# Softmax by column blocks, a fused pass for both norms, row sums in two banks and another order of the G/H products

## The chip, the cores and the metric

The kernel runs on one core of a Trainium2 chip. The metric is the device time of one execution in microseconds (us). TensorE (PE) does the matmuls and PEld its weight loads, VectorE (DVE) and ScalarE (ACT) the elementwise work, GpSimd (POOL) issues most loads. Spans in a profile are some 2 us shorter than the device time of the same run.

## The reference

```python
qn = q / (norm(q, axis=1) + 1e-6); kn = k / (norm(k, axis=1) + 1e-6)   # q, k, v: 4 x 6016 x 256
s = kn.transpose(0, 2, 1) @ qn / tau                                   # 256 x 256 per batch
a = exp(s - max(s)); a /= a.sum(-1) + 1e-9
x = (v @ a).reshape(24064, 256)
out = (sigmoid(x @ w_gate) * (x @ w_val)) @ w_out                      # 256 -> 1536 -> 256
```

The kernel never forms x. It multiplies the small matrix `a` into the weights, G = a w_gate and H = a w_val, once per batch, and then runs a gated MLP from v directly.

## The kernel before

A batch is cut into 12 blocks (ci) of up to 512 tokens, a block into 12 slots (f), each of two gate and two value matmuls (the prediction calls the slots of the first block GLU blocks). Scores, norms, softmax and G/H of the next batch are put into the slots of the present one ("side work"); those of batch 0 run ahead of everything. The parts that matter:

```python
psg = pool("psg", 2, space=PSUM)      # ps_gate: two banks
psv = pool("psv", 2, space=PSUM)      # ps_val: two banks
pso = pool("pso", 2, space=PSUM)
pss = pool("pss", 1, space=PSUM)      # scores of the next batch: one bank
psm = pool("psm", 1, space=PSUM)      # norms, row sums and G/H products: one bank
# ...
def scale_k(b):                       # two passes of 128x256
    for j in range(CB):
        nc.vector.tensor_tensor(out=x, in0=x, in1=s["rk"], op=ALU.mult)
def exps(b):                          # the query norm goes in as the scale
    for j in range(CB):
        nc.scalar.activation(out=s["e"][:, j, :], in_=s["x"][:, j, :], func=ACT.Exp, bias=shift, scale=s["r"][:, j : j + 1])
# ... side work of a transition (next batch n, during blocks 10 and 11)
at(10 * FC + 1, norms_inv, n)
at(10 * FC + 2, spread_k, n)          # four matmuls that spread the key norms over rows: ps_rk
for j in range(CB):
    at(10 * FC + 1, copy_s, n, j)     # scores out of their bank
at(10 * FC + 4, scale_k, n)
at(10 * FC + 11, exps, n)
at(11 * FC + 0, sums, n)              # row sums into psm
for i in range(len(gh_order)):
    at(11 * FC + i, gh, n, i)         # twelve G/H products, all through psm
```

In a slot the order on TensorE is gate (2 matmuls), value (2), 4 matmuls of the previous block's output (in blocks 9 and 10 of batches 0 to 2 they come in one go at the end of the block), then the side work. The value product is evicted by one DVE pass, hT = ps_val x g_sb.

Of the kernel before, what the change touches and what calls it, by code (L numbers as in the profile page):

```python
# [9 lines left out]
FP32 = mybir.dt.float32  # L10
BF16 = mybir.dt.bfloat16
ACT = mybir.ActivationFunctionType
ALU = mybir.AluOpType
# [4 lines left out]
def kernel(  # L18
# [68 lines left out]
    def mm(out, lhsT, rhs, start, stop, **kw):  # L87
        nc.tensor.matmul(out, lhsT=lhsT, rhs=rhs, start=start, stop=stop, **kw)  # L88
# [74 lines left out]
    def squares(b, t0, nt, which, engine):  # L163
        src = qk[b, t0][which]
        sq = sqpool.tile([P, TPC, C], BF16, tag=f"sq{which}", name=f"sq{which}")
        if engine is nc.scalar:
            nc.scalar.activation(out=sq[:, :nt, :], in_=src[:, :nt, :], func=ACT.Square)  # L167
        else:
            engine.tensor_tensor(  # L169
                out=sq[:, :nt, :], in0=src[:, :nt, :], in1=src[:, :nt, :], op=ALU.mult  # L170
            )
        return sq

    def norm_mms(ps, sqs, nt, first, last):

        for w, sq in enumerate(sqs):
            for u in range(nt):
                for j in range(CB):
                    mm(
                        ps[:, w * CB + j : w * CB + j + 1],  # L180
                        sq[:, u, ds(j * P, P)],
                        ones_bf[:, 0:1],
                        start=(first and w == 0 and u == 0 and j == 0),
                        stop=(last and u == nt - 1),
                        skip_group_check=True,
                    )
# [59 lines left out]
            s["x"] = attp.tile([P, CB, C], FP32, tag="x", name="x_sb")  # L246
        nc.vector.tensor_copy(out=s["x"][:, j, :], in_=s["s"][:, j, :])

    def scale_k(b):
        s = st[b]  # L250
        for j in range(CB):
            x = s["x"][:, j, :]
            nc.vector.tensor_tensor(out=x, in0=x, in1=s["rk"], op=ALU.mult)  # L253

    def exps(b):
        s = st[b]
        s["e"] = attp.tile([P, CB, C], BF16, tag="e", name="e_sb", bufs=2)
        for j in range(CB):
            nc.scalar.activation(
                out=s["e"][:, j, :],  # L260
                in_=s["x"][:, j, :],
                func=ACT.Exp,
                bias=shift,
                scale=s["r"][:, j : j + 1],
            )

    def sums(b):
        s = st[b]
        ps_r = psm.tile([P, CB], FP32, tag="m", name="ps_r")
        for i in range(CB):  # L270
            for j in range(CB):
                mm(
                    ps_r[:, i : i + 1],
                    s["e"][:, j, ds(i * P, P)],
                    ones_bf[:, 0:1],
                    start=(i == 0 and j == 0),
                    stop=(j == CB - 1),
                    skip_group_check=True,
                )
        r = attp.tile([P, CB], FP32, tag="rrow", name="rrow", bufs=2)  # L280
        nc.vector.tensor_scalar(out=r, in0=ps_r, scalar1=1e-9, scalar2=None, op0=ALU.add)  # L281
        nc.vector.reciprocal(r, r)
        s["rrow"] = r
        s["gh"] = [
            [ghpool.tile([P, CB, FG], BF16, tag=f"{n}{fg}", name=f"gh_{n}{fg}") for fg in range(NFG)]
            for n in ("G", "H")
        ]

    gh_order = [(fg, w, i) for fg in range(NFG) for w in range(2) for i in range(CB)]

    def gh(b, n, pl=None, tag=None, act=0):
        s = st[b]
        fg, w, i = gh_order[n]
        ps = (pl or psm).tile([P, FG], FP32, tag=tag or "m", name="ps_gh")
        for j in range(CB):
            mm(
                ps,
                s["e"][:, j, ds(i * P, P)],
                w_sb[w][fg][:, j, :],
                start=(j == 0),  # L300
                stop=(j == CB - 1),
            )
        dst = s["gh"][w][fg][:, i, :]
        r = s["rrow"][:, i : i + 1]
        if n % 2 == act:
            nc.scalar.activation(out=dst, in_=ps, func=ACT.Copy, scale=r)  # L306
        else:
            nc.vector.tensor_scalar(out=dst, in0=ps, scalar1=r, scalar2=None, op0=ALU.mult)  # L308
# [1 line left out]

    vts = {}

    def transpose_v(b, ci, ps=None):

        t0, nt = groups[ci]
        v_sb = vs.pop((b, ci))
        vT = vtpool.tile([P, TPC * CB, P], BF16, tag="vT", name="vT")
        flat = v_sb[:, :nt, :].rearrange("p t c -> p (t c)")
        if ps is None:
            nc.sync.dma_start_transpose(out=vT[:, : nt * CB, :], in_=flat)  # L320
        else:
            for n in range(nt * CB):
                nc.tensor.transpose(
                    out=ps[:, n, :], in_=flat[:, ds(n * P, P)], identity=ident_bf
                )
            nc.vector.tensor_copy(out=vT[:, : nt * CB, :], in_=ps[:, : nt * CB, :])
        vts[b, ci] = vT.rearrange("p (u cb) n -> p cb u n", cb=CB)

    hts = {}
# [61 lines left out]
    for g in range(last0 + 2):  # L391
        if g <= last0:
            t0, nt = groups0[g]
            sq[g] = (
                squares(0, t0, nt, 0, nc.vector),
                squares(0, t0, nt, 1, nc.vector if g == last0 else nc.scalar),
            )
            for u in range(nt):
                score(0, t0, u)
        if g >= 1:  # L400
            norm_mms(ps_n0, sq.pop(g - 1), groups0[g - 1][1], g == 1, g == last0 + 1)
    st[0]["n"] = ps_n0
    norms_sqrt(0)
    nc.scalar.preload_act_table(ACT.Exp)
# [2 lines left out]
    copy_s(0, 1)  # L407
    busy(12)
    spread_k(0)
    busy(10)  # L410
    scale_k(0)
    transpose_v(0, 0, psv.tile([P, TPC * CB, P], BF16, tag="v", name="ps_tp"))
    exps(0)
    nc.scalar.preload_act_table(ACT.Sigmoid)
    sums(0)
    for n in range(4):
        gh(0, n, *((psg, "g"), (psv, "v"))[n % 2], act=1)


    def side_work(b):  # L420

        side = {}

        def at(slot, fn, *a):
            side.setdefault(divmod(slot, FC), []).append((fn, a))

        for ci in range(NCH):
            nb, nci = (b, ci + 1) if ci + 1 < NCH else (b + 1, 0)
            lb, lci = (b, ci + 2) if ci + 2 < NCH else (b + 1, ci + 2 - NCH)
            if (nb, nci) == (0, 1):  # L430
                at(7, lambda: transpose_v(0, 1, psm.tile([P, TPC * CB, P], BF16, tag="m", name="ps_tp")))
            elif nb < B:
                at(ci * FC + 2, transpose_v, nb, nci)
            if lb < B:
                at(ci * FC + 0, load_v, lb, lci)
        n = b + 1
        if n == B:
            return side
        first, last = (14 if b == 0 else 0), 9 * FC
        for g, (t0, nt) in enumerate(groups):  # L440
            s0 = first + g * (last - first) // NCH
            at(max(0, s0 - 20), load_qk, n, t0, nt)
            for u in range(nt):
                at(first + (t0 + u) * (last - first) // NT, score, n, t0, u)
            if g == 0:
                at(s0, acc_start, n)
            for i, (fn, w) in enumerate(((acc_square, 0), (acc_add, 0), (acc_square, 1), (acc_add, 1))):
                at(s0 + 1 + 2 * i, fn, n, g, w)
        at(9 * FC + 10, norms_mm, n)
        at(9 * FC + 11, norms_sqrt, n)  # L450
        at(10 * FC + 1, norms_inv, n)
        at(10 * FC + 2, spread_k, n)
        for j in range(CB):
            at(10 * FC + 1, copy_s, n, j)
        at(10 * FC + 4, scale_k, n)
        at(10 * FC + 11, exps, n)
        at(11 * FC + 0, sums, n)
        for i in range(len(gh_order)):
            at(11 * FC + i, gh, n, i)
        return side  # L460


# [1 line left out]
    for b in range(B):  # L464
        side = side_work(b)
        for ci in range(NCH):
            block = b + 1 < B and ci in (9, 10)
            for f in range(FC):
                glu(b, ci, f)
                flush()  # L470
                if prev is not None and not block:
                    out_mms(*prev, f * TPC, (f + 1) * TPC)
                for fn, a in side.get((ci, f), ()):
                    fn(*a)
                if (b, ci) == (0, 0) and f < len(gh_order) - 4:
                    gh(0, 4 + f, pso, "o", act=1)
            if prev is not None and block:
                for s in range(TPC):
                    out_mms(*prev, s * FC, (s + 1) * FC)
                    flush()  # L480
            prev = (b, ci)
# [38 lines left out]
```

## Time and profile before

| | before |
|---|---|
| time, median of the first 3 runs | 840.12 us |
| same kernel, all its later runs beside the experiments | 838.78 to 841.92 us |
| profiled span | 838.0 us |
| PE / DVE / ACT busy | 97% / 68% / 47% |

The prediction shows the views that carry the argument. A busy row of PE is drawn over the start of the next one: a pair of 512-column matmuls is 0.59 us long, though the next pair starts after 0.433 us.

### The profile page before, as it was taken

How to read it: one execution, taken by the hardware profiler on the slowest of the kernel's cores; microseconds unless marked ns; L12 is line 12 of the kernel's file. 1: busy time of each engine (PE TensorE's matmuls, PEld its weight loads, DVE VectorE, ACT ScalarE, POOL GpSimd, SP SyncE). 2: the span in 40 equal slices, each digit the busy share in tenths (PEclk: the TensorE clock that was granted, in tenths of full speed). 3: DMA queues.
4: the chain of work that ended last, by engine and by line, in shares of the span. 5: the costliest groups of instructions: out<-in, count | busy, mean ns of one | idle time of the engine just before them, and what ended most of it. 6: DMA issues, size and time to landing. Idle time of an engine off the chain costs nothing.

```text
span 838.0 us, 14001 instructions
## 1 busy us (share of the span) xinstructions
PE 817.0 (97%) x5338; PEld 506.6 (60%) x5338; DVE 566.3 (68%) x977; ACT 390.6 (47%) x640; POOL 83.2 (10%) x159
## 2 busy tenths in 40 slices
PE   5899999999999999999999999999999999999998
PEld 4646666665666666665565666666566556665666
DVE  2377777776667777777656777777756666666664
ACT  4554444445644444444554444444654444444442
POOL 5532100002011100000210020000000000000000
PEclk9799999999999999999999999999999999999999
DMA  9999624226655443223864453223222422322211
GB/s 209 206 205 186 124 51 89 61 51 136 125 102 107 101 102 63 54 51 85 153 132 83 92 118 80 51 73 67 60 48 51 95 51 73 78 50 65 49 36 69
DMA packets 78739, 77.18 MB, mean 92 GB/s; under 512 B 50769, under 2 KB 55633, under 8 KB 78673
## 3 DMA queue, kind: packets, MB, share of 16 engines
q0 software_dynamic: 23920, 38.81, 28.0%
q1 hardware_dynamic: 54608, 36.97, 15.8%
q8 instruction: 41, 0.67, 0.3%
q10 hardware_dynamic: 144, 0.52, 0.2%
q14 instruction: 26, 0.20, 0.1%
HBM read 78.64 MB, written 24.64 MB: 123 GB/s over the span
## 4 chain that ended last, share of the span: by engine, by line
PE 91%; DMA 3%; DVE 2%; ACT 1%; issue 1%; POOL 0%; ACTq 0%; POOLq 0%
PE ps_o L88 29%; PE ps_gate L88 28%; PE ps_val L88 28%; PE ps_s L88 4%; DMA k_sb<-in_k_dram 3%; PE ps_gh L88 2%; DVE hT L351 1%; ACT g_sb L350 1%; PE ps_rk L88 0%; DVE out_sb L377 0%; ACT gh_H L306 0%; PE ps_n L88 0%; DVE gh_H L308 0%; DVE gh_G L308 0%; DVE x_sb L253 0%
## 5 line engine op out<-in xcount | busy, mean ns | idle before, releaser
L351 DVE TENSOR_TENSOR hT<-ps_val,g_sb 128x512 bf16<-128x512 f32 (+1 forms) x576 | 391.1, 679 | 219.9 <-ACT g_sb L350 216.3
L350 ACT ACTIVATE g_sb<-ps_gate 128x512 bf16<-128x512 f32 (+1 forms) x576 | 338.8, 588 | 399.8 <-PE ps_gate L88 387.3
L88 PE MATMUL ps_val<-vT,gh_H 128*128 128x512 bf16 (+1 forms) x1152 | 338.0, 375 | 0.5
L88 PE MATMUL ps_gate<-vT,gh_G 128*128 128x512 bf16 (+1 forms) x1152 | 337.5, 375 | 0.0
L88 PE MATMUL ps_o<-w_out_sb,hT 128*128 128x256 bf16 x2256 | 326.2, 273 | 0.0
L88 PEld LDWEIGHTS <-hT 128*128 128x128 bf16 x2256 | 220.7, 98 | 124.8
L88 PEld LDWEIGHTS <-gh_H 128*128 128x128 bf16 x1152 | 112.7, 98 | 132.9 <-ACT gh_H L306 1.5
L88 PEld LDWEIGHTS <-gh_G 128*128 128x128 bf16 x1152 | 112.5, 98 | 37.4 <-ACT gh_G L306 0.3
L377 DVE COPY out_sb<-ps_o 128x256 f32<-128x256 f32 x188 | 78.1, 415 | 20.9 <-PE ps_o L88 20.9
L106 POOL DMA_DIRECT2D v_sb<-in_v_dram x48 | 25.6, 534 | 631.7 <-DMA vT<-v_sb 466.0
L88 PE MATMUL ps_s<-k_sb,q_sb 128*128 128x256 bf16 x376 | 72.4, 296 | 13.1 <-ACT k_sb L128 6.8
L88 PEld LDWEIGHTS <-q_sb 128*128 128x128 bf16 x376 | 39.1, 104 | 20.8 <-issue 7.1
L169 DVE TENSOR_TENSOR sq<-q_sb 128x1024 bf16<-128x1024 bf16 (+3 forms) x46 | 30.4, 661 | 20.7 <-PE ps_n L88 17.4
L207 DVE TENSOR_TENSOR acc<-acc,sq 128x1024 bf16<-128x1024 bf16 (+1 forms) x66 | 44.2, 669 | 0.0
L97 POOL DMA_DIRECT2D q_sb<-in_q_dram x48 | 26.4, 549 | 15.6 <-DMA q_sb<-in_q_dram 5.5
L97 POOL DMA_DIRECT2D k_sb<-in_k_dram x48 | 26.1, 545 | 13.6 <-DMA k_sb<-in_k_dram 8.4
L169 DVE TENSOR_TENSOR sq<-k_sb 128x1024 bf16<-128x1024 bf16 (+2 forms) x34 | 22.4, 658 | 0.0
L167 ACT ACTIVATE sq<-k_sb 128x1024 bf16<-128x1024 bf16 (+1 forms) x12 | 12.2, 1021 | 15.6 <-DMA k_sb<-in_k_dram 12.6
L88 PE MATMUL ps_gh<-w_gate,e_sb 128*128 128x512 bf16 x48 | 14.1, 378 | 1.6 <-DVE rrow L281 1.2
L88 PE MATMUL ps_gh<-w_val,e_sb 128*128 128x512 bf16 x48 | 14.1, 379 | 0.4
L88 PEld LDWEIGHTS <-e_sb 128*128 128x128 bf16 x112 | 9.9, 97 | 6.8 <-issue 3.2
L306 ACT ACTIVATE gh_G<-ps_gh,rrow 128x512 bf16<-128x512 f32 x12 | 8.2, 687 | 9.7 <-PE ps_gh L88 9.6
(46 smaller groups left out, 101.6 us busy)
## 6 DMA issues: line engine op xcount, KB each, us to landing
out_dram<-out_sb SPq DMA_DIRECT2D x44, 512.0 KB, 2.8
v_sb<-in_v_dram POOLq DMA_DIRECT2D x44, 256.0 KB, 3.9
q_sb<-in_q_dram POOLq DMA_DIRECT2D x43, 256.0 KB, 6.3
k_sb<-in_k_dram POOLq DMA_DIRECT2D x43, 256.0 KB, 7.8
out_dram<-out_sb SPq DMA_DIRECT2D x4, 384.0 KB, 2.4
w_gate<-in_moe_w_gate_dram POOLq DMA_DIRECT2D x3, 256.0 KB, 6.9
w_val<-in_moe_w_val_dram POOLq DMA_DIRECT2D x3, 256.0 KB, 7.6
w_out_sb<-in_moe_w_out_dram POOLq DMA_DIRECT2D x1, 768.0 KB, 12.6
```

The lines of the kernel that those rows point to most:

```text
L88: nc.tensor.matmul(out, lhsT=lhsT, rhs=rhs, start=start, stop=stop, **kw)
L97: nc.gpsimd.dma_start(out=tl[:, :nt, :], in_=rows(src, b)[:, t0 : t0 + nt, :])
L106: nc.gpsimd.dma_start(out=v_sb[:, :nt, :], in_=rows(v, b)[:, t0 : t0 + nt, :])
L167: nc.scalar.activation(out=sq[:, :nt, :], in_=src[:, :nt, :], func=ACT.Square)
L169: engine.tensor_tensor(out=sq[:, :nt, :], in0=src[:, :nt, :], in1=src[:, :nt, :], op=ALU.mult)
L207: nc.vector.tensor_tensor(out=acc[:, :nt, :], in0=acc[:, :nt, :], in1=st[b]["sq", w][:, :nt, :], op=ALU.add)
L306: nc.scalar.activation(out=dst, in_=ps, func=ACT.Copy, scale=r)
L350: nc.scalar.activation(out=g_sb[:, :n], in_=ps_gate[:, :n], func=ACT.Sigmoid)
L351: nc.vector.tensor_tensor(out=hts[b, ci][:, f, :n], in0=ps_val[:, :n], in1=g_sb[:, :n], op=ALU.mult)
L377: nc.vector.tensor_copy(out=out_sb[:, s, :], in_=ps)
```

## The change

The intent: let the first G/H products of batch 0 start after half of the softmax, apply both inverse norms in one DVE pass, keep the row sums out of the way of the products, and issue the products ahead of the blocks that need them. The diff, cut to its core:

```diff
-    def scale_k(b):
+    def scale_k(b, i):
         for j in range(CB):
-            x = s["x"][:, j, :]
-            nc.vector.tensor_tensor(out=x, in0=x, in1=s["rk"], op=ALU.mult)
+            x = s["x"][:, j, ds(i * P, P)]
+            nc.vector.scalar_tensor_tensor(out=x, in0=x, scalar=s["r"][:, j : j + 1],
+                in1=s["rk"][:, ds(i * P, P)], op0=ALU.mult, op1=ALU.mult)
-    def exps(b):
+    def exps(b, i):                    # one column block, no scale operand
-    def sums(b):
+    def sums(b, i, pl=psm, tag="m"):   # one column block, in a bank of its own
-    gh_order = [(fg, w, i) for fg in range(NFG) for w in range(2) for i in range(CB)]
+    gh_order = [(fg, w, i) for fg in range(NFG) for i in range(CB) for w in range(2)]
 # ... transpose_v: the copy of the transposed v
-            nc.vector.tensor_copy(out=vT[:, : nt * CB, :], in_=ps[:, : nt * CB, :])
+            half = nt * CB // 2
+            nc.vector.tensor_copy(out=vT[:, :half, :], in_=ps[:, :half, :])
+            (nc.scalar.copy if late is None else late)(vT[:, half : nt * CB, :], ps[:, half : nt * CB, :])
 # ... start: six products ahead of the GLU instead of four, then one per slot; the last
 #     squares on ACT and DVE instead of DVE alone; 16 warm-up matmuls instead of 22
 # ... transitions
-        at(10 * FC + 2, spread_k, n)
         for j in range(CB):
-            at(10 * FC + 1, copy_s, n, j)
-        at(10 * FC + 4, scale_k, n)
-        at(10 * FC + 11, exps, n)
-        at(11 * FC + 0, sums, n)
+            at(10 * FC + 2, copy_s, n, j)
+        at(10 * FC + 4, spread_k, n)
+        for i in range(CB):
+            at(10 * FC + 6, scale_k, n, i)
+            at(10 * FC + 11, exps, n, i)
+            at(11 * FC + 0, sums, n, i, *((psm, "m"), (pss, "s"))[i])
         for i in range(len(gh_order)):
-            at(11 * FC + i, gh, n, i)
+            at(11 * FC + min(i + 1, FC - 1), gh, n, i, *((psm, "m"), (pss, "s"))[i % 2])
```

In the transitions the products now alternate between two banks.

More of the change, by code (lines that the diff above doesn't have):

```diff
@@ L172, in squares, with norm_mms @@
         return sq
-    def norm_mms(ps, sqs, nt, first, last):
-        for w, sq in enumerate(sqs):
+    def norm_mms(ps, sqs, nt, first, last, order=(0, 1)):
+        for w in order:
+            sq = sqs[w]
             for u in range(nt):
@@ L182, in norm_mms @@
                         ones_bf[:, 0:1],
-                        start=(first and w == 0 and u == 0 and j == 0),
+                        start=(first and w == order[0] and u == 0 and j == 0),
                         stop=(last and u == nt - 1),
@@ L247, in copy_s @@
         nc.vector.tensor_copy(out=s["x"][:, j, :], in_=s["s"][:, j, :])
-    def scale_k(b):
+    def scale_k(b, i):
         s = st[b]
         for j in range(CB):
-            x = s["x"][:, j, :]
-            nc.vector.tensor_tensor(out=x, in0=x, in1=s["rk"], op=ALU.mult)
-    def exps(b):
-        s = st[b]
-        s["e"] = attp.tile([P, CB, C], BF16, tag="e", name="e_sb", bufs=2)
-        for j in range(CB):
-            nc.scalar.activation(
-                out=s["e"][:, j, :],
-                in_=s["x"][:, j, :],
-                func=ACT.Exp,
-                bias=shift,
-                scale=s["r"][:, j : j + 1],
-            )
@@ L267, in sums @@
-    def sums(b):
-        s = st[b]
-        ps_r = psm.tile([P, CB], FP32, tag="m", name="ps_r")
-        for i in range(CB):
-            for j in range(CB):
-                mm(
-                    ps_r[:, i : i + 1],
-                    s["e"][:, j, ds(i * P, P)],
-                    ones_bf[:, 0:1],
-                    start=(i == 0 and j == 0),
-                    stop=(j == CB - 1),
-                    skip_group_check=True,
-                )
-        r = attp.tile([P, CB], FP32, tag="rrow", name="rrow", bufs=2)
+            x = s["x"][:, j, ds(i * P, P)]
@@ new lines, in scale_k @@
+            nc.vector.scalar_tensor_tensor(
+                out=x,
+                in0=x,
+                scalar=s["r"][:, j : j + 1],
+                in1=s["rk"][:, ds(i * P, P)],
+                op0=ALU.mult,
+                op1=ALU.mult,
+            )
+    def exps(b, i):
+        s = st[b]
+        e = attp.tile([P, CB, P], BF16, tag=f"e{i}", name=f"e_sb{i}", bufs=2)
+        nc.scalar.activation(
+            out=e, in_=s["x"][:, :, ds(i * P, P)], func=ACT.Exp, bias=shift
+        )
+        s.setdefault("e", []).append(e)
+        s.setdefault("rrow", [])
@@ L281, in sums @@
+    def sums(b, i, pl=psm, tag="m"):
+        s = st[b]
+        ps_r = pl.tile([P, 1], FP32, tag=tag, name="ps_r")
+        for j in range(CB):
+            mm(ps_r, s["e"][i][:, j, :], ones_bf[:, 0:1], j == 0, j == CB - 1)
+        r = attp.tile([P, 1], FP32, tag=f"rrow{i}", name="rrow", bufs=2)
         nc.vector.tensor_scalar(out=r, in0=ps_r, scalar1=1e-9, scalar2=None, op0=ALU.add)
         nc.vector.reciprocal(r, r)
-        s["rrow"] = r
-        s["gh"] = [
+        s["rrow"].append(r)
@@ L285, in sums, with gh_tiles @@
+    def gh_tiles(b):
+        st[b]["gh"] = [
             [ghpool.tile([P, CB, FG], BF16, tag=f"{n}{fg}", name=f"gh_{n}{fg}") for fg in range(NFG)]
@@ L287, in sums, with gh @@
         ]
-    gh_order = [(fg, w, i) for fg in range(NFG) for w in range(2) for i in range(CB)]
-    def gh(b, n, pl=None, tag=None, act=0):
+    gh_order = [(fg, w, i) for fg in range(NFG) for i in range(CB) for w in range(2)]
+    def gh(b, n, pl=None, tag=None, act=None):
         s = st[b]
@@ L297, in gh @@
                 ps,
-                s["e"][:, j, ds(i * P, P)],
+                s["e"][i][:, j, :],
                 w_sb[w][fg][:, j, :],
@@ L303, in gh @@
         dst = s["gh"][w][fg][:, i, :]
-        r = s["rrow"][:, i : i + 1]
-        if n % 2 == act:
+        r = s["rrow"][i]
+        if act if act is not None else n % 2 == 0:
             nc.scalar.activation(out=dst, in_=ps, func=ACT.Copy, scale=r)
@@ L311, with transpose_v @@
     vts = {}
-    def transpose_v(b, ci, ps=None):
+    def transpose_v(b, ci, ps=None, late=None):
         t0, nt = groups[ci]
@@ L393 @@
             t0, nt = groups0[g]
-            sq[g] = (
-                squares(0, t0, nt, 0, nc.vector),
-                squares(0, t0, nt, 1, nc.vector if g == last0 else nc.scalar),
-            )
+            engines = (nc.vector, nc.scalar) if g < last0 else (nc.scalar, nc.vector)
+            sq[g] = [squares(0, t0, nt, w, engines[w]) for w in range(2)]
             for u in range(nt):
@@ L400 @@
         if g >= 1:
-            norm_mms(ps_n0, sq.pop(g - 1), groups0[g - 1][1], g == 1, g == last0 + 1)
+            norm_mms(ps_n0, sq.pop(g - 1), groups0[g - 1][1], g == 1, g == last0 + 1, (0, 1) if g <= last0 else (1, 0))
     st[0]["n"] = ps_n0
@@ L409 @@
     spread_k(0)
-    busy(10)
-    scale_k(0)
-    transpose_v(0, 0, psv.tile([P, TPC * CB, P], BF16, tag="v", name="ps_tp"))
-    exps(0)
-    nc.scalar.preload_act_table(ACT.Sigmoid)
-    sums(0)
-    for n in range(4):
-        gh(0, n, *((psg, "g"), (psv, "v"))[n % 2], act=1)
+    busy(4)
+    scale_k(0, 0)
+    scale_k(0, 1)
+    late = []
+    transpose_v(
+        0, 0, psv.tile([P, TPC * CB, P], BF16, tag="v", name="ps_tp"), lambda *a: late.append(a)
+    )
+    exps(0, 0)
+    exps(0, 1)
+    nc.scalar.copy(*late.pop())
+    gh_tiles(0)
+    sums(0, 0)
+    gh(0, 0, psg, "g", act=False)
+    gh(0, 1, psv, "v", act=True)
+    nc.scalar.preload_act_table(ACT.Sigmoid)
+    sums(0, 1, pss, "s")
+    gh(0, 2, psg, "g", act=False)
+    gh(0, 3, psv, "v", act=False)
+    gh(0, 4, pso, "o", act=True)
+    gh(0, 5, pso, "o", act=False)
     def side_work(b):
@@ L451, in side_work @@
         at(10 * FC + 1, norms_inv, n)
-        at(10 * FC + 2, spread_k, n)
         for j in range(CB):
-            at(10 * FC + 1, copy_s, n, j)
-        at(10 * FC + 4, scale_k, n)
-        at(10 * FC + 11, exps, n)
-        at(11 * FC + 0, sums, n)
+            at(10 * FC + 2, copy_s, n, j)
[4 more added lines that the diff above has]
+            at(11 * FC + 0, sums, n, i, *((psm, "m"), (pss, "s"))[i])
+        at(11 * FC + 0, gh_tiles, n)
         for i in range(len(gh_order)):
-            at(11 * FC + i, gh, n, i)
+            at(11 * FC + min(i + 1, FC - 1), gh, n, i, *((psm, "m"), (pss, "s"))[i % 2])
         return side
@@ L474 @@
                     fn(*a)
-                if (b, ci) == (0, 0) and f < len(gh_order) - 4:
-                    gh(0, 4 + f, pso, "o", act=1)
+                if (b, ci) == (0, 0) and f < len(gh_order) - 6:
+                    gh(0, 6 + f, pso, "o")
             if prev is not None and block:
```

## The prediction

> **What bounds the kernel now.** I read the page first: engine shares, then the chain that ended last.
>
> ```profile
> span 838.0 us, 14001 instructions
> PE 817.0 (97%) x5338; PEld 506.6 (60%) x5338; DVE 566.3 (68%) x977; ACT 390.6 (47%) x640; POOL 83.2 (10%) x159
> PE 91%; DMA 3%; DVE 2%; ACT 1%; issue 1%; POOL 0%; ACTq 0%; POOLq 0%
> ```
>
> TensorE is busy 97% of the span and carries 91% of the chain. Idle are 838.0 - 817.0 = 21 us in all, so nothing that leaves the matmuls as they are can win more than 2.5%. Next I asked in which stretches those 21 us lie (columns: stretch in us, its length, then busy us and count for PE, PEld, DVE, ACT, POOL, then granted clock, DMA share, GB/s).
>
> ```profile
> 0.00:31.57 31.57, 18.50 (x224) 14.77 (x225) 8.09 (x14) 12.89 (x12) 16.17 (x35) 0.85 1.05 208
> 35.87:41.00 5.13, 4.58 (x47) 3.04 (x46) 3.81 (x11) 4.53 (x7) 2.38 (x5) 1.00 1.24 205
> 41.00:54.00 13.00, 12.73 (x63) 5.56 (x63) 9.23 (x15) 8.26 (x14) 4.48 (x9) 1.00 1.23 206
> 230.00:270.00 40.00, 39.73 (x252) 24.41 (x251) 27.72 (x48) 18.62 (x34) 5.84 (x11) 1.00 0.58 109
> 670.00:818.00 148.00, 148.00 (x915) 89.24 (x913) 91.40 (x152) 68.08 (x115) 2.65 (x5) 1.00 0.23 57
> ```
>
> 13.1 us are lost before 31.57 us, where the chain waits for k: loads that the change doesn't touch. 3.65 us are lost after 818, in the last store and eviction, untouched too. The softmax part of the first batch (35.9 to 54) and the three later batch transitions (near 209 to 226, 411 to 428, 613 to 630) are all that the change reaches. So the question is a sum of tenths of a microsecond, taken from the timeline and the chain of the start and of one transition.
>
> Start, timeline and chain (start us, length us, what):
>
> ```profile
> 37.38 0.75 DVE L253 TENSOR_TENSOR x_sb<-x_sb,ps_rk 128x256 f32<-128x256 f32 x2 [0.55 <-PE ps_rk L88]
> 37.83 1.09 ACT L259 ACTIVATE e_sb<-x_sb,shift,r 128x256 bf16<-128x256 f32 x2 [0.45 <-DVE x_sb L253]
> 39.07 1.02 PE L88 MATMUL ps_gh<-w_gate,e_sb 128*128 128x512 bf16 x4
> 40.98 0.10 PEld L88 LDWEIGHTS <-gh_G 128*128 128x128 bf16 x1 [0.30 <-ACT gh_G L306]
> 46.48 0.70 ACT gh_H L306
> 52.41 0.70 ACT gh_H L306
> ```
>
> The first G/H product must wait for both exponentials (38.92) and starts at 39.07. Then three evictions hold TensorE: at 40.98, and twice where the G/H product that block f of the GLU needs is issued just before that block (46.48, 52.41).
>
> First transition:
>
> ```profile
> 210.19 0.71 PE L88 MATMUL ps_rk<-ident_f,r 128*128 128x128 f32 x4 [0.41 <-DVE r L224]
> 213.47 0.74 DVE L253 TENSOR_TENSOR x_sb<-x_sb,ps_rk 128x256 f32<-128x256 f32 x2
> 214.13 1.28 DVE L351 TENSOR_TENSOR hT<-ps_val,g_sb 128x512 bf16<-128x512 f32 x2
> 214.86 0.59 PE L88 MATMUL ps_val<-vT,gh_H 128*128 128x512 bf16 x2
> 225.71 0.59 PE L88 MATMUL ps_gh<-w_gate,e_sb 128*128 128x512 bf16 x2 [0.40 <-DVE rrow L281]
> ```
>
> TensorE waits 0.41 us for the inverse norms and 0.40 us for the row sums to leave the single bank. A third loss shows no wait entry: pairs of 512-column matmuls start every 0.433 us, the gate pair before started at 214.19, so ps_val was due at 214.62 and started at 214.86. That 0.24 us is the 0.74 us of scaling, which pushed the hT eviction to the end of the two ps_val buffers. The wait lists of the three transitions agree to 0.1 us.
>
> **What the skill says.** "TensorE: Matmul & The Clock Gate", section "Wait — 56ns, not 53.3ns?", gives 215.7 ns from start to start for warm 512-column matmuls; a pair would be 0.431 us, and the trace has 0.433. "ScalarE: Activation LUTs", section "What ACT_TABLE_LOAD costs", gives 186 ns + 0.833 ns per element and about 93 ns more per pointer operand. For the old exponential (256 elements, scale and bias as pointers) that is 585 ns; the trace has 592. The new one has one pointer: estimate 592 - 93, say 0.50 us. "VectorE: DVE Perf Modes", the section on the TRN2 errata, has (N+151)/0.96 ns for an fp32 tensor_tensor: 424 ns at 256 (the trace: 412), 291 at 128. It gives no figure for the fused form. The second of two back to back costs 0.33 us in the trace, 0.06 more than its 256 cycles.
>
> **The change part by part.**
>
> 1. Scaling. Two 128x256 passes (0.75 us) become four 128x128 fused ones. By the spacing above a 128-column step is 128/0.96 + 63 = 0.20 us. The pointer scalar costs something: the trace has 742 ns for a 512-column tensor_scalar with a pointer and 690 for a tensor_tensor, so 0.05. Estimate: 0.34 for the first, 0.22 for each next, 1.0 us for four: 0.25 more on DVE.
>
> 2. Start. The first column block is scaled at 37.38 + 0.34 + 0.22 = 37.94, its exponential runs 37.97 to 38.47, its two row-sum matmuls go at 38.52 and the first G product at 38.58, against 39.07: 0.49 us earlier. The second exponential ends near 38.97, before its sums are wanted at 39.45. Six G/H products now precede the GLU. The Sigmoid table load (1.28 us) moves behind one ACT eviction, to 40.33 to 41.61, so it no longer holds an eviction that the first gate pair needs. By the chain of evictions (DVE 0.74, ACT 0.69) gate 0 starts at 41.24 when its second G half is ready at 41.05, and H at 41.75 is just in time. I expect one new small wait, about 0.24 us: product 6 needs the bank of product 4, which ACT frees only at 42.3. All twelve products are then issued by f = 5, ahead of f = 4 and f = 8 that need them, so the three eviction waits go, some 0.3 us each (e.g. 46.01 to 47.61 holds 1.60 us for 1.30 us of work). Check by work: from the first G product to the end of GLU block 8 there are 12 x 0.433 + 9 x 0.866 + 0.45 for a transposition = 13.44 us, from 39.07 it took until 53.54, 14.47. After: 38.58 + 13.44 + 0.06 (second sums) + 0.24 = 52.32. Gain: 1.2 us.
>
> 3. Last squares on two engines: the last ps_n matmuls run at their own pace (12 in 0.55 to 0.58 us), so 0 to 0.1; I count 0. Six warm-up matmuls fewer: off the chain, TensorE is waiting there; 0. The half copy of vT to ACT: 0, beside other work.
>
> 4. Each of three transitions. Copies move to slot 2 and the spread to slot 4: the 0.41 wait goes, as r is ready two slots earlier. The copies (0.72 us) now delay hT, but the 0.55 us of spread matmuls give the buffers time; I walked hT(3) to 212.14 against ps_val(5) at 212.34: no stall. The scaling at slot 6 is 0.25 longer in one piece: its stall grows from 0.24 to about 0.45 to 0.5. The 0.40 for the row sums goes: the first product comes a slot (1.1 us) later than its sums. Sum: 0.41 + 0.24 + 0.40 - 0.45 = 0.6 us, 1.8 us for three.
>
> 5. Two products in the last slot: the bank of the second must be free for the next batch's first score, 1.3 us later; DVE needs some 0.95. No cost. The other order of products, and the smaller exponentials beside the block of out matmuls: 0.
>
> Sum: 1.2 + 1.8 = 3.0 us. 840.1 - 3.0 = 837.1.
>
> **The rivals.** (a) *The DVE pass takes back what was won.* If the fused form runs at 0.30 us a step instead of 0.22, four cost 1.25 us, the stall at slot 6 becomes 0.7 to 0.8 us and a transition wins 0.3; the total falls to about 2 us, 838. For it: hT repeats every 0.866 us and takes 0.69, so DVE has 0.17 us to spare a slot, and only two ps_val buffers. Against: the same walk of the buffers overestimated the stall of before (0.37 for the 0.24 measured).
> (b) *The start is bound elsewhere.* ACT has a dense row there (two exponentials, half a copy, an eviction, a table load, 3.6 us); if g_sb 0 or the bank of product 4 slips further, the 1.2 falls to 0.6. Total 838. For it: the ACT idle gaps are nil from 37.97 to 42.9 in my walk.
> (c) *The loads of the start.* k lands at 31.57 and everything follows. If an altered pace of the other engines moved those loads by half a microsecond, it would be as large as a third of my sum, either way. Against: squares and scores up to there are unchanged. The three runs of before spread over 0.7 us, so noise of that kind is 0.3.
> (d) *TensorE is the bound throughout and nothing shows*: the losses named are in the chain one by one, so this could only be if each were replaced. About 839.5 to 840.
>
> **Range and chances.** Centre 837.1. Rivals (a) and (b) together give 838.7; both estimates too careful (stall 0.2 at slot 6, no wait for product 6) gives 836.1; adding 0.4 for noise, 835.6 to 839.0. Faster by over 2% means below 823.3, which would take most of the 21 us of idle time, of which the change reaches about four: chance 0.005. Slower by over 2% would need 17 us of new waits, some 4 us in each stage: 0.005.
>
> **What would show it.** In the changed trace: the first ps_gh near 38.6 instead of 39.07 and gate 9 near 52.3 instead of 53.54; no wait of TensorE for gh_G or gh_H at the start; no entries of ps_rk for r and ps_gh for rrow in the transitions; a ps_val gap of 0.4 to 0.5 us one block or two after the four fused passes; the four passes at 1.0 us in the timeline, the exponentials near 0.50. PE busy time should hardly change. The prediction is wrong if the fused pass is far off 0.22 us a step, if moving the copies to slot 2 makes its own stall, or if the loads end at another time.

## The result, and the profile after

The changed kernel takes 834.77 us (median of 6 runs, 834.38 to 836.2) against 839.64 us (6 runs, 839.29 to 840.18). The ratio of the fast runs is 0.9946 (95% interval 0.9933 to 0.9958). The class "within 2%" was right; the size was not: 837.1 was forecast, and 834.77 lies below the range of 835.6 to 839.0. Some 4.5 to 4.9 us came off, not 3.0.

The page of the changed kernel, the same lines as before and one group:

```profile
span 832.8 us, 14005 instructions
PE 813.2 (98%) x5322; PEld 506.0 (61%) x5332; DVE 568.6 (68%) x993; ACT 390.8 (47%) x642; POOL 82.9 (10%) x159
PE 93%; DMA 4%; DVE 1%; issue 0%; POOL 0%; ACT 0%; POOLq 0%
```

Less of the chain lies on DVE and ACT; TensorE is even more the bound.

Start, timeline of the changed kernel:

```profile
36.45 1.12 DVE L255 SCALAR_TENSOR_TENSOR x_sb<-x_sb,r,ps_rk 128x128 f32<-128x128 f32 x4 [0.56 <-PE ps_rk L88]
37.09 1.03 ACT L268 ACTIVATE e_sb<-x_sb,shift 128x256 bf16<-128x256 f32 x2 [0.62 <-DVE x_sb L255]
37.72 0.38 PE L88 MATMUL ps_gh<-w_gate,e_sb 128*128 128x512 bf16 x1
40.38 0.59 PE L88 MATMUL ps_gh<-w_val,e_sb 128*128 128x512 bf16 x2 [0.29 <-DMA w_val<-in_moe_w_val_dram]
51.31 0.41 DVE L328 COPY vT<-ps_tp 128x512 bf16<-128x512 bf16 x1
51.76 0.59 ACT L329 COPY vT<-ps_tp 128x512 bf16<-128x512 bf16 x1 [1.09 <-DVE vT L328]
52.89 0.59 PE L88 MATMUL ps_gate<-vT,gh_G 128*128 128x512 bf16 x2 [0.25 <-ACT g_sb L353]
```

The first product starts at 37.72 instead of 39.07, more than the 0.49 us expected. The waits for gh_G and gh_H are gone. Two new ones are there: the sixth product waits for its weights (40.38), and the gate matmuls wait at 52.89, because the second half of the vT copy, on ACT, starts only when the DVE half has ended, and holds the sigmoids behind it.

First transition, the instructions that answer to those of before:

```profile
210.29 0.61 PE L88 MATMUL ps_rk<-ident_f,r 128*128 128x128 f32 x4
213.46 1.11 DVE L255 SCALAR_TENSOR_TENSOR x_sb<-x_sb,r,ps_rk 128x128 f32<-128x128 f32 x4
214.49 1.28 DVE L354 TENSOR_TENSOR hT<-ps_val,g_sb 128x512 bf16<-128x512 f32 x2
215.23 0.59 PE L88 MATMUL ps_val<-vT,gh_H 128*128 128x512 bf16 x2 [0.45 <-DVE hT L354]
224.90 0.38 PE L88 MATMUL ps_gh<-w_gate,e_sb 128*128 128x512 bf16 x1
```

ps_rk and ps_gh wait for nothing. The scaling takes 1.11 us in one piece instead of 0.74, and ps_val, due at 214.62, starts at 215.23.

To add up what each piece is worth, I compared the starts of the same gate matmul in both traces. This needs no idle column: it says how far the changed kernel is ahead at each place.

| place | lead of the changed kernel, us | change |
|---|---|---|
| first ps_rk | 0.93 | |
| first G/H product | 1.35 | +0.42 |
| batch 0, block 0, gate of slot 9 | 1.77 | +0.42 |
| same, slot 11 (after the vT copy) | 1.06 | -0.71 |
| transition: ps_rk | | +0.68 |
| transition: scaling | | +0.24 - 0.61 |
| transition: row sums | | +0.53 |
| transition: two more places among the products | | +0.30 +0.30 |
| each transition in all | | +1.42 |
| last gate matmul | 5.32 | |

The leads of the three transitions agree to 0.02 us. The first line is odd: nothing of the change lies ahead of it but the last squares and the order of their sums. And "two more places" is a term that the prediction does not have at all. In the kernel before, one of them looks like this:

```profile
230.95 0.41 DVE L377 COPY out_sb<-ps_o 128x256 f32<-128x256 f32 x1
231.28 0.74 DVE L308 TENSOR_SCALAR gh_H<-ps_gh,rrow 128x512 bf16<-128x512 f32 x1
232.08 0.59 PE L88 MATMUL ps_gh<-w_gate,e_sb 128*128 128x512 bf16 x2
```

The copy of an output tile gets ahead of the eviction of a product on DVE; the single bank comes free at 232.02, and the next product, which could have started at 231.77 (0.433 us after the output matmuls at 231.34), starts at 232.08. No row carries a wait mark, since the row of the output matmuls before (0.60 us) is drawn over most of the gap.

As for the first line, the granted clock in the 3 us ahead of the first ps_rk differs. Columns: stretch, length, busy us and count of PE, PEld, DVE, ACT, POOL, then clock, DMA share, GB/s. Before:

```profile
31.90:34.90 3.00, 3.00 (x40) 2.29 (x39) 0.46 (x2) 1.46 (x2) 2.99 (x5) 0.50 1.22 206
```

After:

```profile
31.90:34.90 3.00, 2.94 (x60) 2.68 (x60) 0.98 (x4) 2.10 (x3) 2.70 (x4) 1.00 1.21 206
```

Half clock before, full clock after, and 60 matmuls instead of 40 in the same time. Ten profiles have no matmuls added at the start; from the landing of the last k to the square root of the norms they take 1.08 to 1.09 us where the clock was full by 30.7 us (three of them, the changed kernel among these), 1.49 where it was full by 32.8 or 32.9 (two), 1.78 where by 33.3 (one) and 2.24 to 2.36 where by 34.7 to 35.4 (four, before among them). Old and new starts with a late clock agree to 0.12 us there, so splitting the last squares over two engines is worth no more than that.

### The profile page after: what moved, and what is told of

It is laid out like the page before. It is cut to its first block, busy times and chain, and to the rows that moved or that the text cites. A ratio compares the mean times of both kernels' runs of the same rounds, so it can differ in the third digit from the quotient of the medians.

```text
span 832.8 us, 14005 instructions
## 1 busy us (share of the span) xinstructions
PE 813.2 (98%) x5322; PEld 506.0 (61%) x5332; DVE 568.6 (68%) x993; ACT 390.8 (47%) x642; POOL 82.9 (10%) x159
## 4 chain that ended last, share of the span: by engine, by line
PE 93%; DMA 4%; DVE 1%; issue 0%; POOL 0%; ACT 0%; POOLq 0%
PE ps_o L88 30%; PE ps_gate L88 29%; PE ps_val L88 29%; PE ps_s L88 4%; DMA k_sb<-in_k_dram 3%; PE ps_gh L88 2%; DMA w_val<-in_moe_w_val_dram 1%; DVE hT L354 1%; ACT g_sb L353 0%; DVE x_sb L255 0%; PE ps_rk L88 0%; PE ps_n L88 0%; POOL q_sb L97 0%; POOL w_gate L137 0%; POOL k_sb L97 0%
## 5 line engine op out<-in xcount | busy, mean ns | idle before, releaser
L169 DVE TENSOR_TENSOR sq<-q_sb 128x1024 bf16<-128x1024 bf16 (+2 forms) x45 | 30.1, 670 | 19.0 <-PE ps_n L88 18.2
L307 ACT ACTIVATE gh_G<-ps_gh,rrow 128x512 bf16<-128x512 f32 x22 | 15.1, 687 | 13.3 <-PE ps_gh L88 9.1
L309 DVE TENSOR_SCALAR gh_H<-ps_gh,rrow 128x512 bf16<-128x512 f32 x23 | 17.1, 743 | 1.8 <-PE ps_gh L88 1.6
L88 PE MATMUL ps_gh<-w_val,e_sb 128*128 128x512 bf16 x45 | 13.6, 379 | 0.5 <-DMA w_val<-in_moe_w_val_dram 0.3
```

What stands on the lines that cost most here:

```text
L88: nc.tensor.matmul(out, lhsT=lhsT, rhs=rhs, start=start, stop=stop, **kw)
L169: engine.tensor_tensor(out=sq[:, :nt, :], in0=src[:, :nt, :], in1=src[:, :nt, :], op=ALU.mult)
L307: nc.scalar.activation(out=dst, in_=ps, func=ACT.Copy, scale=r)
L309: nc.vector.tensor_scalar(out=dst, in0=ps, scalar1=r, scalar2=None, op0=ALU.mult)
```

## The experiments

Theory: the transitions carry the gain, by four terms read from starts (spread +0.68, scaling -0.37, sums +0.53, bank +0.60 us), and the full clock of the start is chance. Rival: the start, with its clock, made the extra gain, and the transitions gave the 1.8 us of the prediction. Kernels named b_ are the kernel before with an edit, a_ the changed kernel with an edit. The times of before beside them were 839.74 to 840.44 us (medians of 7 runs).

### b_two_banks: the products in two banks, nothing else

```diff
-            at(11 * FC + i, gh, n, i)
+            at(11 * FC + i, gh, n, i, *((pss, "s"), (psm, "m"))[i % 2])
```

> The kernel before, with one thing of the change: in the transitions the G/H products alternate between two banks, the first one not in the bank of the row sums. Theory A (the transitions carry the gain, through the single bank): the wait for the row sums (0.53 us by the starts of the matmuls) and two waits of 0.30 us for an eviction in the single bank go, 1.13 us a transition, 3.4 us in all: some 836.2 us, ratio 0.996. Theory B (the gain of the change came from the start, above all from full clock 5 us earlier there): 0 to 0.5 us, 839.3. Theory C, as in the prediction (only the 0.40 for the row sums): 1.2 us, 838.4.

Measured: 836.3 us (835.54 to 837.53), ratio 0.9954 (0.9937 to 0.9971). The leads over before are +0.53, +0.29 and +0.29 us in each transition, 3.4 us in all; the last gate matmul is 3.25 us ahead, since the start was 0.10 us later than before's. Timeline:

```profile
225.50 0.38 PE L88 MATMUL ps_gh<-w_gate,e_sb 128*128 128x512 bf16 x1
225.62 0.15 DVE L281 TENSOR_SCALAR rrow<-ps_r 128x2 f32<-128x2 f32 x1
230.86 0.74 DVE L308 TENSOR_SCALAR gh_H<-ps_gh,rrow 128x512 bf16<-128x512 f32 x1
231.36 0.59 PE L88 MATMUL ps_gh<-w_gate,e_sb 128*128 128x512 bf16 x2
```

The first product starts before the row sums are read, and a later one while the product before it is being evicted. Theory A holds; a one-line edit gives most of the change's gain.

### b_late_spread: copies to slot 2, spread to slot 4, scaling to slot 6, nothing else

```diff
-        at(10 * FC + 2, spread_k, n)
-            at(10 * FC + 1, copy_s, n, j)
-        at(10 * FC + 4, scale_k, n)
+            at(10 * FC + 2, copy_s, n, j)
+        at(10 * FC + 4, spread_k, n)
+        at(10 * FC + 6, scale_k, n)
```

> The kernel before, with one thing of the change: in the transitions the copies of the scores move to slot 2, the spread of the key norms to slot 4, the two old scaling passes to slot 6. Theory A: 0.68 us a transition go (0.57 by which the spread started late and 0.11 by which its four matmuls ran longer when not prefetched), 2.0 us in all: some 837.6 us. As predicted, by the idle time of the trace: 0.41 us each, 1.2 us, 838.4. Rival: the copies at slot 2 hold hT and give it back as a ps_val stall: 0 to 0.5 us.

Measured: 838.17 us (837.25 to 838.27), ratio 0.9973 (0.9958 to 0.9988); lead +0.66 us per transition, 2.05 us at the end with 0.06 of it from the start. The time alone doesn't tell the theory (2.0 us) from the prediction's 1.2 us; the trace does: the wait that the idle column put at 0.41 us cost some 0.67. The stall of the scaling moved along and kept its 0.24 us.

### b_two_moves: both edits together

> The kernel before with the edits of b_two_banks and b_late_spread together and nothing else: whole-width softmax, two old scaling passes, old order of products, old start. Theory: the two add up, 1.12 + 0.68 = 1.80 us a transition, 5.4 us in all: some 834.7 us, ratio 0.9936, no slower than the whole change, so that the fused passes, the column blocks and the other order win nothing net in the transitions and take back 0.37 us in each. Rival: the waits overlap or a new one comes in their place, and the sum is 4 us or less (836.1).

Measured: 835.32 us (833.82 to 836.88), ratio 0.9949 (0.9927 to 0.9972). From the second block of batch 0 to the first gate of batch 3 it takes 585.57 us; before takes 590.96, the changed kernel 586.69. The two add up (5.4 us), and in that stretch the two moves alone beat the whole change by 1.1 us, three times the 0.37 us that the fused passes cost. So the column blocks and the other order of the products, the visible part of the change, win nothing net in the transitions. Its two longer runs (836.54, 836.88) have mean clocks of 0.988 and 0.990, its two shorter ones 0.992, as one expects if the old start makes the spread: in its profile the first ps_rk was at 35.95 us, in that of before at 36.66, with not one instruction changed ahead of it.

### a_split_scale: the second scaling block at slot 8

```diff
-            at(10 * FC + 6, scale_k, n, i)
+            at(10 * FC + 6 + 2 * i, scale_k, n, i)
```

> The changed kernel, with the second column block scaled at slot 8 instead of slot 6. Theory: the four fused passes in one piece (1.11 us) hold hT so long that ps_val waits 0.61 us; in two pieces of some 0.55 us DVE recovers between them, the stall falls to 0 to 0.15 us each: 1.0 to 1.8 us in all against the changed kernel, some 833.3 us. Rival: the stall is not of the scaling (ps_val would wait the same): no difference, 834.7.

Measured: 832.84 us (832.63 to 834.02), ratio 0.9914 (0.9899 to 0.993); lead over the changed kernel +0.51 us in each transition. Timeline:

```profile
213.34 0.60 DVE L255 SCALAR_TENSOR_TENSOR x_sb<-x_sb,r,ps_rk 128x128 f32<-128x128 f32 x2
215.07 0.60 DVE L255 SCALAR_TENSOR_TENSOR x_sb<-x_sb,r,ps_rk 128x128 f32<-128x128 f32 x2
215.45 0.59 PE L88 MATMUL ps_val<-vT,gh_H 128*128 128x512 bf16 x2
```

Two pieces of 0.60 us, and of the 0.61 us stall 0.10 stays. The stall comes from doing the scaling in one long piece.

### a_wide_pass: two fused passes of 256 columns in the transitions

> The changed kernel, with the transitions' scaling as two fused passes of 128x256 instead of four of 128x128 (the start keeps four). If the fused form costs as much as a tensor_tensor and only the number of passes made the scaling long, two take some 0.8 us and the ps_val stall falls from 0.61 to 0.25 to 0.35 us: 0.8 to 1.1 us in all, 833.8 us. If the fused form is itself slow, two take 1.0 us or more and the stall stays above 0.5 us: 834.5 us.

Measured: 834.63 us (833.61 to 835.33), ratio 0.9939 (0.9924 to 0.9953); lead +0.25 us in each transition. Timeline:

```profile
213.15 0.86 DVE L268 SCALAR_TENSOR_TENSOR x_sb<-x_sb,r,ps_rk 128x256 f32<-128x256 f32 x2
214.67 0.59 PE L88 MATMUL ps_val<-vT,gh_H 128*128 128x512 bf16 x2 [0.20 <-DVE hT L362]
```

Two fused passes take 0.86 us, two tensor_tensor passes 0.74, four narrow fused ones 1.11. One wide fused pass takes 472 ns, a tensor_tensor 412: 60 ns for the pointer scalar and the second operation together. Two thirds of the longer scaling came from the number of passes, one third from the form. The time moved less than the 0.76 us in the traces; against the ratio of the changed kernel (0.9946) it is inside the intervals.

### a_whole_copy: the copy of the transposed v in one piece on DVE

```diff
-            half = nt * CB // 2
+            half = nt * CB if late is None else nt * CB // 2
 # ... the DVE copy of the first half, unchanged: at slot 7 it now takes all 1024 columns
-            (nc.scalar.copy if late is None else late)(vT[:, half : nt * CB, :], ps[:, half : nt * CB, :])
+            if late is not None:
+                late(vT[:, half : nt * CB, :], ps[:, half : nt * CB, :])
```

> The changed kernel, with the copy of the transposed v of block 1 (slot 7 of block 0) in one piece on DVE as before, not half on ACT. Theory: the ACT half waits for the DVE half (1.09 us idle) and holds g_sb, so the gate matmuls stall by 0.71 us; with the whole on DVE a stall of about 0.3 us stays, so 0.4 us less than the changed kernel, about 834.4 us. Rival: the DVE queue alone makes the stall: it stays 0.7 us or grows.

Measured: 834.32 us (833.63 to 835.62), ratio 0.993 (0.991 to 0.9951); the whole 0.71 us came back, not 0.4. The gate matmuls follow every 0.87 us through the copy (51.40, 52.26, 53.13, 53.99). Halving the copy over two engines made it worse than one engine: the halves ran one after the other, and the second stood before the sigmoids.

### a_warm and b_warm: TensorE kept busy through the waits of the start

```diff
+        if 3 <= g <= 10:
+            busy(12)                # 12 matmuls of 128 columns after a group of scores
```

> The changed kernel with 12 matmuls of 128 columns after each of the groups 3 to 10 of the first scores, so that TensorE works through the waits for the loads. Theory: the clock at which the last groups run (half until 35.4 us in the profile of before, full from 30.5 us in that of the changed kernel) is chance of phase and not of the change; kept busy, the clock is full from some 25 us on in every run, the first ps_rk starts 1.0 to 1.3 us after its k has landed less than with a late clock, and the runs, which lay at 834.4 to 834.9 and 836.0 to 836.2, all lie at 834.5 or below with a smaller spread. Rival 1: the clock of these 5 us is of no account, since the weights' load holds the start anyway: 834.8 with the same spread. Rival 2: the added matmuls run at half clock and push the scores behind the loads: 836 or more.

> The kernel before with the same added matmuls. Theory: it too gets the full clock early, wins about 0.9 us (it waits for no weights there) and comes to some 839 us; against the changed kernel with the same matmuls the difference is then without the chance of the clock, 4.3 (transitions) + 0.1 to 0.4 (start), so 4.4 to 4.7 us. If the clock had been the reason of the change's extra gain, the difference would be near the 3.0 us that were predicted.

Measured: a_warm 835.5 us (835.42 to 835.66), ratio 0.994; b_warm 840.11 us (839.61 to 840.36), ratio 0.9992 (0.9976 to 1.0009). In the profiled runs the clock is full from 24.2 us on in the one and from 11.0 us in the other. The spread of the changed kernel fell from 1.8 us (6 runs) to 0.24 (4 runs), which agrees with the clock of the start as its cause. The difference of the two, 4.6 us by the medians and 4.68 in the traces, is free of that chance: 4.29 in the transitions, 0.39 in the start, of which 0.10 lies ahead of the first ps_rk, where a_warm's last k landed 0.10 us earlier.

But neither kernel won at the start; the 0.9 us expected for b_warm did not come. The timeline of a_warm has two reasons. The first is the added matmuls themselves:

```profile
32.99 0.83 PE L88 MATMUL ps_busy<-ones_bf 128*128 128x128 bf16 x12
33.66 0.60 PE L88 MATMUL ps_s<-k_sb,q_sb 128*128 128x256 bf16 x4
```

The k of the last group but one landed at 33.00, and its scores stand behind the added matmuls until 33.66; the last scores and squares follow late. From the landing of the last k to the square root it takes 1.70 us (b_warm: 1.71), in the changed kernel with its early clock 1.09. So rival 2 came true in part, at full clock. The second:

```profile
35.29 1.06 POOL L142 DMA_DIRECT2D w_out_sb<-in_moe_w_out_dram  x1
35.57 0.77 DVE L224 TENSOR_SCALAR r<-r 128x4 f32<-128x4 f32 x1 [0.22 <-ACT r L220]
```

Adding 1e-6 to four columns takes 0.16 us in the transitions. Here it lasts 0.77 us and ends at 36.34, GpSimd's issue of the load of w_out at 36.35. The same holds in b_warm (36.44 for both), b_late_spread (36.23 and 36.27) and five more profiles: the pass ends with that issue, to 0.04 us. The Trainium skill's "SBUF — State Buffer", section "Who interferes with whom", says that a VectorE tensor_scalar in a two-port mode and a GpSimd instruction exclude each other for a whole instruction, whoever starts first; these ends agree with that, though no run here shows the ports themselves or the mode of the pass. Not every issue holds it, though. In the changed kernel the pass starts inside the shorter issue of a v load and is not held:

```profile
34.99 0.57 POOL L106 DMA_DIRECT2D v_sb<-in_v_dram  x1
35.20 0.17 DVE L224 TENSOR_SCALAR r<-r 128x4 f32<-128x4 f32 x1 [0.22 <-ACT r L220]
```

Three other profiles show the same, and in b_two_moves the pass started 0.02 us after the issue of w_out and took 0.17 us. What in an issue holds the pass stays open. So the added matmuls delayed r by 0.6 us, which brought it to DVE just when the issue of w_out held it for another 0.6.

### a_gh_after: the sixth product and later ones behind the GLU

> The changed kernel with four G/H products ahead of the GLU instead of six; the fifth follows GLU block 0, the sixth and seventh block 1, then one per block. Theory: the sixth product waits for its weights, which land at 40.34 us, and holds the first gate matmul; moved behind, GLU block 0 starts near 39.6 to 40.4 us, and 0.3 to 0.6 us is won where the clock was early, 0.2 where it was late: 834.4 us. Rival: the evictions of the first four products hold the gate instead (DVE has three of them and two reciprocals in a row): no gain, 834.8.

Measured: 835.55 us (834.67 to 837.08), ratio 0.9942. It wins nothing. Counted from the first ps_rk, the gate of slot 9 comes at 16.32 us, in the changed kernel at 15.88. The rival was right: with fewer products ahead, the first gate pair waits for DVE.

```profile
41.24 0.39 PE L88 MATMUL ps_gate<-vT,gh_G 128*128 128x512 bf16 x1 [0.41 <-DVE gh_G L309]
```

### a_both_sums: both row sums ahead of the first product

> The changed kernel with the row sums of both column blocks ahead of the first G/H product at the start, so that this product waits for the second exponential as before the change. Theory (what the blocks win at the start is held up again by the load of the weights): the first product starts 0.4 to 0.5 us later, but the sixth one waits that much less for its weights at 40.34 us; over all 0 to 0.3 us slower, 834.8 to 835.1 us. Rival (the prediction's step 2): the whole 0.49 us is lost, 835.3 us.

Measured: 835.6 us (834.38 to 836.03), ratio 0.9938 (0.9923 to 0.9954). By time it can't be told from the changed kernel. In the traces, from the first ps_rk: the first product at 2.50 us instead of 1.99, the gate of slot 1 at 6.73. The changed kernel has 6.37 there, and 6.22 in a_whole_copy and a_warm, where no product waited for weights. So my theory fell: the weights take back only 0.15 us of the 0.51 that the column blocks win at the start, and the 0.36 left is real.

### best_warm and best_warm_w: what the experiments point to

Both: the changed kernel with the scaling at slots 6 and 8, the whole copy on DVE, and 12 added matmuls after groups 3 to 8. The second also issues the next load of v ahead of that of w_out.

> The changed kernel with the second block's scaling at slot 8, the whole copy of the transposed v on DVE, and 12 added matmuls after groups 3 to 8 of the first scores. From the earlier runs: a_warm 835.5 less 0.51 x 3 less 0.71, 833.3 us. In a_warm the addition of 1e-6 to the norms (four columns on DVE) took 0.77 us instead of 0.17 and ended in the 10 ns in which GpSimd ended issuing the load of w_out; where r comes before that issue it should not be held (0.6 us less, 832.6), where it comes during it, it is held.

> As best_warm, but GpSimd issues the next v load first and the load of w_out after it. Theory: what holds the four-column DVE pass is GpSimd's long issue (1.03 us for w_out); with the short one (0.56 us) in its place the pass ends at the latest with that, so some 35.8 instead of 36.3 us: 0 to 0.5 us against best_warm. Rival: the pass is slow for another reason (its place in the queue, the clock), and nothing changes; or w_out then lands too late for the first ps_o and the start waits, slower by some us.

Measured: 832.04 us (831.98 to 833.75), ratio 0.9908 (0.9892 to 0.9925), and 832.14 us (831.94 to 833.25), ratio 0.9913 (0.9898 to 0.9927). Both beat the changed kernel; between them there is no difference. In the profile of the second the four-column pass took 0.17 us and ps_rk started at 35.47; but r came before the long issue there, inside a short one of v (34.73 to 35.29) that did not hold it, so the run does not decide whether the order of the two loads matters. Its last two groups have no matmuls added, and from the last k to the square root it takes 1.09 us again. In the profile of the first the clock fell to half from 32.1 to 39.0 us, after the last added matmuls, and that was its slowest run (833.75).

## Why the prediction was wrong

The bound, the class and the direction of every transition term that it had were right. The sum failed, in its last two lines: "Sum: 1.2 + 1.8 = 3.0 us."

- **Step 4, "0.41 + 0.24 + 0.40 - 0.45 = 0.6 us, 1.8 us for three"**, is the step that failed. Measured were 0.68 - 0.37 + 0.53 + 0.60 = 1.44 us (1.42 and 1.43 by the whole transition in the two pairs of traces, 4.29 for three in a_warm against b_warm).
  - Two terms were taken from the idle column, 0.41 and 0.40. From start to start they are 0.68 and 0.53 (b_late_spread, b_two_banks). The row of a matmul pair is 0.16 us longer than its pace of 0.433, so each idle entry was short by about that (0.57 and 0.53 us late by the starts); and the spread matmuls ran 0.55 us instead of 0.44 when they had just been waited for. I had used the pace for ps_val in the same paragraph, and not for these two.
  - One term was missing: the other two waits for the single bank, 0.30 us each. They carry no mark in the trace, and I looked only for marks. The diff gave the bank away in its last line; I read that line as a question of whether it cost something ("No cost").
  - The stall of the scaling was to grow from 0.24 to 0.45 or 0.5 and grew to 0.61. Four fused passes took 1.11 us instead of 1.0. Rival (a) named this with the right mechanism; it cost 0.37 us a transition and was outweighed.
  - The copies at slot 2 made no stall, as walked through.
- **Step 2, start, 1.2 us.** With the clock out of the way (a_warm against b_warm) it is 0.39. The parts that I had worked out came near: counted from the first ps_rk, the first product comes 0.43 us earlier (0.49 predicted), the gate of slot 9 1.00 (1.2); an exponential takes 507 ns (0.50 predicted). The check by work took 53.54, the drawn end of a row, for the start of gate 9, which is 53.38: the same error of 0.16 us as in step 4. The wait of product 6 for its bank turned into one for its weights in the profiled run. What broke it is **step 3, "The half copy of vT to ACT: 0, beside other work"**: it cost 0.71 us (a_whole_copy).
- **Rival (c)**, the noise of the start, was put at 0.3 us. Its size is over 1 us, and its main cause is not the loads but the clock: the last k landed at 33.46 to 33.90 us in the ten profiles without added matmuls, but from there to the square root it took 1.08 to 2.36 us. In the profiled pair this chance favoured the changed kernel by some 0.9 us; in the times it did not decide, for 4.6 us also separate the kernels with a clock kept full.
- The range of 1.5 us downward was too narrow: four terms of a transition, each off by 0.13 to 0.60 us, count three times.

The prediction took the k that landed at 31.57 for the last one of the start, and it left one stretch of its own query out of its table, the one where TensorE looks full and runs at half clock for most of the time:

```profile
31.57:35.87 4.30, 4.25 (x61) 3.35 (x61) 1.59 (x5) 1.69 (x2) 3.92 (x6) 0.55 1.24 205
```

Idle time, the 21 us from which it set its ceiling, does not contain what a half clock costs.

The errors in the start (-0.8) and the transitions (+2.5) partly cancel; 3.0 - 0.8 + 2.5 = 4.7, against 4.6 to 4.7 without the clock. For unprofiled runs the record has the mean clock alone. It agrees: of the 26 runs of before beside the experiments, the five at 0.987 took 840.89 to 841.92 us, the thirteen at 0.991 or more 838.78 to 840.44. When in such a run the clock was low stays open.

## What to carry to other kernels

On an engine whose rows overlap, price a wait by the starts of the instructions around it against their pace, not by the idle column, and look for gaps in the pace where no wait is marked: a single bank can cost 0.3 us again and again without an entry. Where an engine has little to spare per slot and two buffers, cut long side work into pieces over slots. Compare small gains from a fixed instruction onward, since the clock of a start that waits for loads can move a whole run by over 1 us.

## What the Trainium skill lacked or had wrong

- "TensorE: Matmul & The Clock Gate", Part 1, says that about 3.4 us of activity release the clock, that the penalty is below 1% of a typical span, and that no count of cold matmuls should be fitted. It gives no figure for how busy such a stretch must be. In b_late_spread the clock stayed at half from 19.7 to 33.3 us, with matmuls drawn busy for 10.77 of these 13.6 us; it rose for good anywhere from 30.4 to 35.4 us in the ten profiles without added matmuls. That moves a run by over 1 us of 835: below 1%, but a third of what was predicted here. Twelve added 128-column matmuls per group held it in four profiles (from 24.2 us on at the latest), except in best_warm once they had ended.
- "Perfetto Trace Analysis" warns at its head that busy time of matmuls is a bad metric because they are pipelined. It does not say that idle time before a matmul is short for the same reason: 0.41 and 0.40 us of idle cost 0.68 and 0.53 us here, and two waits of 0.30 us left no idle entry at all.
- "VectorE: DVE Perf Modes", section on the TRN2 errata, has no figure for the fused scalar_tensor_tensor. Measured with one PSUM input, fp32: 342 ns at 128 columns, 472 at 256, four of 128 back to back 1.11 us; a tensor_tensor takes 412 at 256, where the page's formula, which it states as exact at 512 and 2048, gives 424.
